# Scores of fourteen attention units on eight 64-row by 32-column tiles instead of two 128-row by 64-column ones

## The chip, the cores and the metric

The kernel runs on one core of one Trainium2 chip. The metric is the time of one execution in microseconds (us), as the median of several runs. One other execution of the same program was profiled; all rows shown here come from it.

## The reference

Four inputs of 576 tokens, eight heads of 64, go through windowed attention and then through two feed-forward layers (512 to 2048 to 512) on the 2304 tokens. Heads 0 to 3 look at the last 32 tokens, heads 4 to 7 at every fourth of the last 128.

```python
rel = pos[:, None] - pos[None, :]
mask_plain = (rel >= 0) & (rel < window)                                   # window 32
mask_dil = (rel >= 0) & (rel < window * dilation) & (rel % dilation == 0)  # dilation 4
scores = np.where(masks, q @ k.T / sqrt(D), -1e9)
attn = exp(scores - max) / (sum + 1e-9);  y = attn @ v      # y: 2304 x 512
h = y @ w_in;   g = where(h > 0, h, exp(min(h, 0)) - 1);   y = g @ w_out
h = y @ w2_in;  g = h * clip(h + 3, 0, 6) / 6;             out = g @ w2_out
```

## The kernel before, in words

**Units.** The attention is cut into 18 units of 128 tokens, all eight heads (`unit`, line 520). A unit has eight blocks `n`: four of the dilated heads (one for each residue), four of the plain heads, each with 32 queries of four heads against a window of 64 keys. A unit is a chain: loads of q, k, v; scores on TensorE into PSUM tile `ps` (`scores`); for units 4 to 17 VectorE adds the mask while it copies to SBUF (`low`), takes the row minimum (`top`), ScalarE exponentiates with the row sums (`expos`), VectorE scales; TensorE turns the result (`turn`, into `pp`); two copies bring it to `pt`; TensorE multiplies with v (`pv`, into `po`); and a copy and a subtraction bring it to `xh`, `xl`, the two halves that the first layer reads (the last six units: one copy to `xw` and a store).

**Zero padding in q.** Heads lie in pairs, a pair's two times 64 dimensions on the 128 partitions. Line 579 issues one matmul for each block and pair `c`: 128 rows, 64 stationary columns (32 queries of the one head with zeros in the other head's rows, then the reverse), 64 moving columns of keys. That is 16 fp32 matmuls in a unit, `c` = 0 on the left half of the array and `c` = 1 on the right half.

**Order of the work.** The kernel is one program written out job by job. `Plan.run` places the jobs: it walks forward in an estimated time, takes for each engine the job that can start first, ties by `key`, and charges each job the cost in its `job(...)` call (scores: 0.071 us x 16 = 1.136). What it decides is fixed in the program: each engine runs its list in order and waits at semaphores. The keys of the first feed-forward layer are spread over three blocks of 512 tokens, whose starts `TB` hold `CFG["AT"]` us for each attention unit (4, 6 and 4 units). The second layer follows with keys counted from `TB[3]`. Units 4 to 7 feed block 1, units 8 to 11 block 2, units 12 to 17 the second layer's first part. All loads and most stores are issued by SyncE's queue.

**PSUM.** Eight banks with names: h0, h1 (the `h` of the first layer), y0 to y3 (its outputs), a0, a1 (attention of units 4 to 17). `ps`, `pp` and `po` of a unit each take one of a0, a1, whichever is free first, and free it when their last reader is done. Each use is a tile of its own in that bank.

**Masks.** GpSimd writes five masks at the start (`make_mask`, `make_masks`). Units whose blocks touch the beginning of an input (4, 5, 9, 13, 14) need more than one and split `low` into runs of blocks with the same mask.

Of the kernel before, what the change touches and what calls it, by code (L numbers as in the profile page):

```python
# [20 lines left out]
P = 128  # L21
# [18 lines left out]
    LAGT=0.23, LAGE=0.07, LAND=1.6,  # L40
    T0=30.0, AT=2.6,
    AHEAD=6,
    LEAD=10.0,
    LAG=12.0,
# [154 lines left out]
def tile_window_attention_two_mlps(  # L199
    ctx: ExitStack,  # L200
    tc: tile.TileContext,
    q_in: bass.AP,
    k_in: bass.AP,
# [40 lines left out]
    minus = at.tile([P, P], BF16, name="minus")  # L244
    mask = at.tile([P, 5, KW], BF16, name="mask")
    NL = 2 * N1
# [273 lines left out]
    def unit(u, key, step):  # L520
# [3 lines left out]
        for n, src, shape, us, dk in (  # L524
            ("q", q_in, [P, 2, NB, KW], 1.3, 0), ("k", k_in, [P, k_in.shape[2]], 1.1, 0),
            ("v", v_in, [P, NB // 2, HH, D], 1.3, CFG["VL"]),
        ):

            pool, ring = (at, n) if not 0 < u < U1 else {
                "q1": (None, "raw"), "q2": (None, "raw"), "k1": (None, "raw")  # L530
            }.get(f"{n}{u}", (w1p, "w1"))

            def load(e, n=n, src=src, shape=shape, pool=pool, ring=ring):
                t[n] = grab(lu[n], shape, F32, f"{n}{u}") if lu[n].tag else take(pool, ring, shape, F32, f"{n}{u}")
                nc.sync.dma_start(out=t[n], in_=src[u])

            ld[n] = job(key - CFG["LEAD"] + dk, load, {"S": 0.42}, (), us, [(RINGS[ring], lu[n])])

        masks = [first_seen(u * QB, S // DIL)] * DIL + [first_seen(u * UN + n * QB, S) for n in range(UN // QB)]
        tags = []  # L540
        for _ in range(3):
            tags.append(bank_tags[0] if u < U1 else "a")
            bank_tags.rotate(-1)
        r = {}

        def bank(k, shape, nm):
            r[nm] = ps.tile(shape, F32, tag=bu[k].tag, name=f"{nm}{u}")
            return r[nm]
# [13 lines left out]
        pe_masks = u < CFG["MPE"]  # L562

        def masked(e):
            pe = bank(0, [P, NB, KW], "ps")
            for n, w, z in runs:
                nc.tensor.matmul(
                    pe[:, n:n + w, :], minus, mask[:, z:z + 1, :].to_broadcast([P, w, KW]), start=(n == 0), stop=False
                )

        def scores(e):
            pe = r["ps"] if pe_masks else bank(0, [P, NB, KW], "ps")
# [69 lines left out]
        def pv(e):  # L642

            po = bank(2, [P, KD, UN], "po")
# [22 lines left out]
        if pe_masks:  # L667
            j0 = job(key - CFG["KM"], masked, {"T": 0.25}, [setup if full else setups], 0, take1)
            bu[0].append(j0)
        j1 = job(  # L670
            key, scores, {"T": 0.071 * 2 * NB},
            [ld["q"], ld["k"], j0 if pe_masks else setups, (LAST["pv"], -9.0) if u == U1 else None],
# [37 lines left out]
        bu[1] += j7  # L710
        j8 = job(key + 0.7, pv, {"T": 0.066 * 2 * NB}, [*j7, ld["v"]], 0, [(RINGS[tags[2]], bu[2])])
        lu["v"].append(j8)
# [51 lines left out]
    def tile1(b, i):  # L764
# [5 lines left out]
        def g1(e):  # L770
            r["h"] = ps.tile([P, T1], F32, tag=hu.tag, name=f"h{b}_{i}")
            gemm1(w_t[0, i, 0], x_t[b], r["h"], i == 0)
# [33 lines left out]
        def g2(e):  # L806
            w, g = w_t[0, i, 1], r["g"]
            for n in range(KD):
                if i == 0:
                    ys[b, n] = ps.tile([P, T1], F32, tag=f"y{n}", name=f"yp{b}_{n}")  # L810
# [279 lines left out]
    def tile_l(t, i):  # L1090
# [13 lines left out]
        def mm(e):  # L1104
            for n in range(KD):
                if i == 0:
                    ys["l", t, n] = ps.tile([P, N1], F32, tag=yu[n].tag, name=f"yl{t}_{n}")
                for s, (a, v) in enumerate(PASSES):
# [30 lines left out]
    def gemm2nd(c, j):  # L1139
# [10 lines left out]
        def mm(k):  # L1150
# [3 lines left out]
            def fn(e):  # L1154
                if b not in r:
                    r[b] = ps.tile([P, N1], F32, tag=bu[b].tag, name=f"c{b}{c}_{j}")
                    if b == "q":
# [119 lines left out]
    def second(c, h, j):  # L1277
# [19 lines left out]
        for n, (k, ka, kb) in enumerate(PASS[h]):  # L1297
# [38 lines left out]
            def mm(e, r=r, k=k, kb=kb, n=n):  # L1336
                if j == 0:
                    for nm in (str(k), HALF[k][0]):
                        if (c, nm) not in half:
                            opened.add((c, nm))  # L1340
                            half[c, nm] = ps.tile([P, 2, EH], F32, tag=mu[nm].tag, name=f"m{c}_{nm}")
                    for i in range(NG):
# [121 lines left out]

    def make_masks(e):
        later(3, QB // 2)

        nc.gpsimd.memset(mask[:, 2], 0.0)
        for h in range(HH):
# [4 lines left out]
            )  # L1474
        nc.gpsimd.memset(mask[:, 4], 1.0)
        nc.gpsimd.affine_select(
            out=mask[:, 4], in_=mask[:, 4], base=WIN + QB // 2 - 1, pattern=[[-1, KW]], channel_multiplier=0, fill=0.0,
            compare_op=ALU.is_ge,
        )
        m = mask[:, 2]  # L1480
        nc.gpsimd.tensor_tensor(out=m, in0=m, in1=mask[:, 4], op=ALU.mult)
        nc.gpsimd.tensor_tensor(out=m, in0=m, in1=mask[:, 0], op=ALU.add)

    def fill(t0, t1):
# [5 lines left out]
        tag = RINGS["h"].take(())  # L1490
        y = ps.tile([P, P], F32, tag=tag, name=f"fill{next(turns)}")
        for _ in range(n):
# [73 lines left out]
def layout(q, k, v, moe_w_in, moe_w_out, moe2_w_in, moe2_w_out):  # L1566
# [11 lines left out]

    r["q"] = np.zeros((nu, 2, D, 2, NB, 2, QB), q.dtype)
    qd = cut(q).reshape(DIL, 2, 2, nu, QB, D).transpose(3, 2, 5, 1, 0, 4)  # L1580
    qp = flat(q).reshape(2, 2, nu, UN // QB, QB, D).transpose(2, 1, 5, 0, 3, 4)
    for e in range(2):
        r["q"][:, e, :, :, :DIL, e] = qd[:, e]
        r["q"][:, e, :, :, DIL:, e] = qp[:, e]
    r["q"] = r["q"].reshape(nu, P, 2, NB, KW)
    kp, kd, vp, vd = before(flat(k)), before(cut(k)), before(flat(v)), before(cut(v))
    r["k"] = np.zeros((nu, P, 2 * (UN + WIN) + 2 * DIL * KW), k.dtype)
    r["v"] = np.zeros((nu, 2, KW, NB // 2, hh, D), v.dtype)
    for u in range(nu):
# [42 lines left out]
```

## Time and profile before

| | |
|---|---|
| median of 3 runs | 829.96 us (829.28 to 830.64) |
| the profiled execution | 829.3 us, of it span of instructions 827.6 us |
| TensorE busy (PE) | 811.6 us, 98% |
| VectorE (DVE) / ScalarE (ACT) / GpSimd (POOL) busy | 636.3 (77%) / 505.5 (61%) / 47.6 us (6%) |
| granted TensorE clock | 1.00 in every stretch asked for |
| DMA | 230.49 MB, 279 GB/s over the span |

PE are matmuls, PEld the loads of their stationary operand, which run beside them. An fp32 matmul leaves two records of each kind. The units lie between 5 and 281 us, the first layer between 29 and 341 us, the second from 330 us on.

### The profile page before, as it was taken

How to read it: one execution, taken by the hardware profiler on the slowest of the kernel's cores; microseconds unless marked ns; L12 is line 12 of the kernel's file. 1: busy time of each engine (PE TensorE's matmuls, PEld its weight loads, DVE VectorE, ACT ScalarE, POOL GpSimd, SP SyncE). 2: the span in 40 equal slices, each digit the busy share in tenths (PEclk: the TensorE clock that was granted, in tenths of full speed). 3: DMA queues.
4: the chain of work that ended last, by engine and by line, in shares of the span. 5: the costliest groups of instructions: out<-in, count | busy, mean ns of one | idle time of the engine just before them, and what ended most of it. 6: DMA issues, size and time to landing. Idle time of an engine off the chain costs nothing.

```text
span 827.6 us, 15806 instructions
## 1 busy us (share of the span) xinstructions
PE 811.6 (98%) x5691; PEld 750.5 (91%) x5691; DVE 636.3 (77%) x1310; ACT 505.5 (61%) x1179; POOL 47.6 (6%) x71
## 2 busy tenths in 40 slices
PE   8899999999999999999999999999999999999998
PEld 7788888888877887999999999999999999999998
DVE  5999898877778787677998675797677896555985
ACT  2999975766676655677786554444555445444452
POOL 2000010001001000100000000100001100002001
PEclk9999999999999999999999999999999999999999
DMA  9999557866888736999779998986999915778323
GB/s 355 408 408 367 195 180 246 271 213 228 261 287 294 243 125 216 397 414 401 266 256 339 392 373 312 400 339 179 343 379 355 389 59 171 255 256 291 96 59 121
DMA packets 89550, 230.49 MB, mean 279 GB/s; under 512 B 9344, under 2 KB 24192, under 8 KB 89472
## 3 DMA queue, kind: packets, MB, share of 16 engines
q1 hardware_dynamic: 89328, 229.35, 77.8%
q8 instruction: 45, 0.74, 0.4%
q14 instruction: 33, 0.27, 0.1%
q10 hardware_dynamic: 144, 0.13, 0.0%
HBM read 163.38 MB, written 66.06 MB: 277 GB/s over the span
## 4 chain that ended last, share of the span: by engine, by line
PE 78%; DMA 10%; DVE 4%; ACT 4%; issue 1%; SPq 1%; DVEq 0%; ACTq 0%
PE m L1353 20%; PE cq L1163 15%; PE h L757 11%; PE yp L812 9%; PE yl L1109 8%; PE cr L1163 7%; PE cp L1163 4%; DMA raw<-in_w_in_dram 3%; DMA w2do<-store__95 2%; ACT s L614 1%; DMA w2do<-stg 1%; PE po L653 1%; PE m_1x L1353 1%; DMA w2di<-store__95 1%; DMA ws_e<-w2de 1%
## 5 line engine op out<-in xcount | busy, mean ns | idle before, releaser
L812 PE MATMUL yp<-ghl,w 128*128 128x512 f32 x576 | 141.0, 393 | 0.0
L812 PEld LDWEIGHTS yp<-ghl,w 128*128 128x128 f32 x576 | 106.6, 188 | 22.6
L757 PE MATMUL h<-xh,w 128*128 128x512 f32 x384 | 125.6, 394 | 0.1
L1163 PE MATMUL cq<-x,ws_i 128*128 128x384 f32 x576 | 113.3, 339 | 0.7 <-ACT t L276 0.6
L1163 PEld LDWEIGHTS cq<-x,ws_i 128*128 128x128 f32 x576 | 100.9, 188 | 1.4 <-ACT t L276 1.1
L1353 PE MATMUL m<-w,gc 128*128 128x256 f32 x792 | 100.2, 281 | 0.0
L1353 PEld LDWEIGHTS m<-w,gc 128*128 128x128 f32 x792 | 97.2, 190 | 0.0
L757 PEld LDWEIGHTS h<-xh,w 128*128 128x128 f32 x384 | 72.0, 188 | 15.5 <-DVE e L790 0.3
L276 ACT CAST gc<-g 128x384 fp32r<-128x384 f32 x96 | 49.2, 514 | 41.8 <-PE m L1353 22.1
L757 PE MATMUL h<-xl,w 128*128 128x512 f32 x192 | 73.3, 389 | 0.0
L276 ACT COPY t<-cq 128x384 f32<-128x384 f32 x96 | 45.7, 476 | 38.9 <-PE cq L1163 38.0
L1209 ACT ACTIVATE g<-t 128x384 f32<-128x384 f32 x72 | 37.8, 525 | 49.0 <-DVE t L1199 49.0
L1109 PE MATMUL yl<-gl,w 128*128 128x384 f32 x384 | 67.4, 334 | 0.0
L1109 PEld LDWEIGHTS yl<-gl,w 128*128 128x128 f32 x384 | 66.7, 188 | 0.0
L279 DVE TENSOR_TENSOR gc<-g,gc 128x384 fp32r<-128x384 f32 x85 | 48.2, 569 | 17.8 <-ACT gc L276 16.6
L276 ACT CAST gc<-gf 128x384 fp32r<-128x384 f32 x72 | 37.0, 514 | 39.7 <-PE m L1353 35.9
L1215 DVE SCALAR_TENSOR_TENSOR g<-g,t 128x384 f32<-128x384 f32 x72 | 40.2, 559 | 26.6 <-ACT g L1209 26.1
L1163 PE MATMUL cr<-x,ws_i 128*128 128x384 f32 x288 | 55.7, 339 | 0.0
L1353 PE MATMUL m<-ws_e,gc 128*128 128x256 f32 x384 | 52.3, 282 | 0.8 <-DMA ws_e<-w2de 0.8
L335 ACT ACTIVATE raw<-raw 128x512 f32<-128x512 f32 x64 | 42.5, 683 | 17.1 <-DMA raw<-in_w_out_dram 11.6
L1199 DVE TENSOR_TENSOR t<-cr,t 128x384 f32<-128x384 f32 x64 | 35.6, 556 | 20.1 <-ACT t L276 17.9
L1163 PEld LDWEIGHTS cr<-x,ws_i 128*128 128x128 f32 x288 | 50.9, 188 | 0.0
(139 smaller groups left out, 1450.6 us busy)
## 6 DMA issues: line engine op xcount, KB each, us to landing
ws_i<-w2di SPq DMA_DIRECT2D x84, 512.0 KB, 5.5
raw<-in_w_in_dram SPq DMA_DIRECT2D x32, 512.0 KB, 8.0
raw<-in_w_out_dram SPq DMA_DIRECT2D x32, 512.0 KB, 6.5
ws_l<-w2dl SPq DMA_DIRECT2D x28, 512.0 KB, 7.3
ws_e<-w2de SPq DMA_DIRECT2D x24, 512.0 KB, 4.3
w2di<-store__95 SPq DMA_DIRECT2D x44, 256.0 KB, 4.8
rhs<-stg SPq DMA_DIRECT2D x28, 384.0 KB, 6.0
x<-rhs SPq DMA_DIRECT2D x28, 384.0 KB, 8.4
```

Of the source, the lines that this page charges most:

```text
L276: (nc.scalar.copy if e == "A" else nc.vector.tensor_copy)(out=out, in_=in_)
L279: ENG[e].tensor_tensor(out=out, in0=in0, in1=in1, op=ALU.subtract)
L335: nc.scalar.activation(out=x, in_=x, func=AF.Prelu, scale=2.0 ** -112, alpha=-2.0 ** 32)
L614: nc.scalar.activation(out=r["s"][:, n, :], in_=x[:, n, :], func=AF.Exp, scale=z, bias=r["mx"][:, n], accum_out=r["sm"][:, n],)
L757: nc.tensor.matmul(h, w[:, a, c * P:(c + 1) * P], x[b][:, c, :], start=n == 0, stop=n == len(steps) - 1,)
L812: nc.tensor.matmul(ys[b, n], w[:, a, n * P:(n + 1) * P], g[:, c, :], start=(i == 0 and s == 0), stop=(i == KF - 1 and s == 2),)
L1109: nc.tensor.matmul(ys["l", t, n], w_t[0, i, 1][:, a, n * P:(n + 1) * P], r["g"][:, v], start=i == 0 and s == 0, stop=i == KF - 1 and s == 2,)
L1163: nc.tensor.matmul(r[b], w[:, a, p * P:(p + 1) * P], x2[c, k, p][:, z, :], start=start and p == 0 and n == 0, stop=p == 1 and n == 2, skip ...
L1199: nc.vector.tensor_tensor(out=r[n], in0=r[b], in1=r[n], op=ALU.add)
L1209: nc.scalar.activation(out=g_t[c, j][:, k, t].rearrange("q i n -> q (i n)"), in_=r[src], func=AF.Relu, bias=3.0)
L1215: nc.vector.scalar_tensor_tensor(out=z, in0=z, scalar=6.0, in1=r[src], op0=ALU.min, op1=ALU.mult)
L1353: nc.tensor.matmul(ms[c, k, i], r["z"][:, a, i * P:(i + 1) * P], w[:, v, :], start=(c, nm) in opened, stop=end and s == 2,)
```

## The change

For units 4 to 17 `scores2`, `low2` and `pv2` take the place of `scores`, `low` and `pv`. Each head's scores are a matmul of its own: 64 rows (that head's dimensions), 32 stationary columns (its 32 queries, no zeros), 64 moving columns, 32 matmuls in a unit. Row half `z` goes with the head of the pair, column quarter `g` with the pair and the block's parity; consecutive matmuls go to the eight tiles (z, g) in turn. The results of the two row halves go to the two banks a0 and a1 at the same partitions, so a unit's scores take both banks at once (a new ring "pair"), half of each. `low2` reads both with one instruction of 512 elements, or, in the five masked units, with four of 128. q of these units has no zeros and is half as large (256 KB in place of 512). Blocks come in another order, so v is laid out in another order and `pv2` writes its 16 matmuls through other strides. GpSimd makes three copies of the first mask and one mixed mask more. All PSUM tiles become areas of one tile `psum_`. The plan is told 0.8 us for the scores (`TS`), 0.45 us more for a masked `low2`, 3.2 us for `make_masks` in place of 2.0, and 2.3 us in place of 2.6 for `AT`.

```diff
-    T0=30.0, AT=2.6,
+    T0=30.0, AT=2.3,
...
-    LEAD=10.0,
+    LEAD=10.0, TS=0.8,
...
+    RINGS["pair"] = Ring([Pair("a0", BANKS["a0"], BANKS["a1"])])
+    psum_ = ps.tile([P, len(BANKS), DM], F32, name="psum_")
...
-            ("q", q_in, [P, 2, NB, KW], 1.3, 0), ...
+            ("q", q0_in, [P, 2, NB, KW], 1.3, 0) if u < U1 else ("q", q_in, [P, 2, NB, QB], 0.65, 0), ...
...
-            tags.append(bank_tags[0] if u < U1 else "a")
+            tags.append(bank_tags[0] if u < U1 else "a" if tags else "pair")
...
+        def scores2(e):
+            pe = r["ps"] = psum_[:, AREA["a0"]:AREA["a0"] + 2, :DM // 2].rearrange("p z (a b) -> p z a b", b=KW)
...
+            for kind in range(2):
+                for m in range(2):
+                    for g in range(2 * 2):
+                        c, n = g // 2, 2 * m + g % 2
+                        w = window(n if kind else DIL + n)
+                        for z in range(2):
+                            rows = slice(z * D, (z + 1) * D)
+                            nc.tensor.matmul(
+                                pe[g * QB:(g + 1) * QB, z, 2 * kind + m, :], t["q"][rows, c, kind * DIL + n, :], w[rows, c],
+                                start=True, stop=True, tile_position=(z * D, g * QB),
+                            )
...
+        def low2(e):
...
+            while n < NB // 2:
+                w = NB // 2 if not any(kinds) else 1
+                m = mask_[:, :w] if w > 1 else mask[:, kinds[n]:kinds[n] + 1]
+                nc.vector.scalar_tensor_tensor(
+                    out=flat(s[:, :, n:n + w]), in0=flat(r["ps"][:, :, n:n + w]), scalar=-SCALE,
+                    in1=m.rearrange("p (a n) k -> p a (n k)", a=1).to_broadcast([P, 2, w * KW]),
+                    op0=ALU.mult, op1=ALU.add,
+                )
+                n += w
...
-            key, scores, {"T": 0.071 * 2 * NB},
+            key, *((scores, {"T": 0.071 * 2 * NB}) if u < U1 else (scores2, {"T": CFG["TS"]})),
...
-            j2 = job(key + 0.1, low, {"D": C["D"](n)}, [j1])
+            j2 = job(key + 0.1, low2 if u >= U1 else low, {"D": C["D"](n) + 0.45 * any(kinds)}, [j1])
...
     def make_masks(e):
+        for n in range(3):
+            nc.gpsimd.tensor_copy(out=mask_[:, n], in_=mask[:, 0])
+        for h in range(HH):
+            rows = slice(h * QB, (h + 1) * QB)
+            nc.gpsimd.tensor_copy(out=mask[rows, 4], in_=mask[rows, 1 - h % 2])
...
-        setups = job(0.0, make_masks, {"P": 2.0})
+        setups = job(0.0, make_masks, {"P": 3.2})
```

## Rows read from the trace of the kernel before

**Rows 1.** The page's first part: busy us (share), instructions, of each engine.
```profile
PE 811.6 (98%) x5691; PEld 750.5 (91%) x5691; DVE 636.3 (77%) x1310; ACT 505.5 (61%) x1179; POOL 47.6 (6%) x71
```
**Rows 2.** Busy time by stretch: length; engines; granted clock; DMA share; GB/s.
```profile
26.00:60.00 34.00, 33.34 (x285) 27.10 (x284) 32.67 (x66) 33.14 (x83) 0.00 (x0) 1.00 1.04 408
60.00:100.00 40.00, 40.00 (x285) 32.55 (x284) 35.70 (x67) 37.72 (x90) 0.00 (x0) 1.00 0.81 290
220.00:285.00 65.00, 62.40 (x469) 50.44 (x468) 48.05 (x106) 44.69 (x132) 5.55 (x7) 1.00 0.83 275
285.00:828.00 543.00, 534.64 (x3458) 523.36 (x3456) 404.52 (x829) 299.14 (x639) 29.41 (x29) 1.00 0.77 277
```
**Rows 3.** PE's waits from 26 to 290 us: total us, times, longest.
```profile
PE po L653 <- DVE pt L276: 1.7, 1, 1.7
PE po L653 <- ACT pt L276: 0.8, 2, 0.4
PE pp L629 <- DVE s L624: 0.5, 2, 0.4
```
**Rows 4.** Line 579 from 28 to 267 us: count; shortest, median, longest ns.
```profile
L579 PE MATMUL ps<-k,q x448: 222/222/270, 28.2 to 266.6; 128*64 128x64 f32 x150
```
**Rows 5.** Timeline around one unit's scores: start us, length us, engine, line.
```profile
74.17 1.01 PEld L579 LDWEIGHTS ps<-k,q 128*64 128x64 f32 x32 [0.35 <-issue]
74.17 1.15 PE L579 MATMUL ps<-k,q 128*64 128x64 f32 x32
...
75.25 0.53 PEld L812 LDWEIGHTS yp<-ghl,w 128*128 128x128 f32 x3
```
**Rows 6.** Timeline of PE, cut at 74.20 us: the burst's first records.
```profile
74.17 0.28 PE L579 MATMUL ps<-k,q 128*64 128x64 f32 x2
```
**Rows 7.** Line 579 in short stretches: PE records in flight (x), then PEld's.
```profile
74.16:74.20 0.04, 0.03 (x2) 0.03 (x2) 1.00 1.25 486
74.20:74.27 0.07, 0.07 (x2) 0.07 (x4) 1.00 1.00 380
74.27:74.30 0.03, 0.03 (x4) 0.03 (x6) 1.00 1.40 546
74.30:74.33 0.03, 0.03 (x4) 0.03 (x6) 1.00 0.85 341
74.33:74.36 0.03, 0.03 (x6) 0.03 (x6) 1.00 1.24 478
```
**Rows 8.** Timeline from 154.5 to 158 us: a unit's end beside the next one's scores.
```profile
154.84 1.15 PE L653 MATMUL po<-pt,v 128*64 128x64 f32 x32
...
155.82 1.10 PE L579 MATMUL ps<-k,q 128*64 128x64 f32 x32
...
156.84 0.68 DVE L660 TENSOR_TENSOR xl<-po,xh 128x512 fp32r<-128x512 f32 x1
```
**Rows 9.** DVE's line 586 by shape: count, busy us, mean ns, idle before.
```profile
L586 DVE SCALAR_TENSOR_TENSOR s<-ps,mask 128x512 f32<-128x512 f32 x9 | 6.1, 683 | 0.9 <-PE ps L579 0.9
L586 DVE SCALAR_TENSOR_TENSOR s<-ps,mask 128x128 f32<-128x128 f32 x2 | 0.6, 277 | 0.0
```
**Rows 10.** Timeline of POOL, the end of the masks.
```profile
7.25 0.30 POOL L1482 TENSOR_TENSOR mask<-mask 128x64 bf16<-128x64 bf16 x1
```
**Rows 11.** DMA issues by line: count, KB each, median us to landing.
```profile
q<-in_q_dram SPq DMA_DIRECT2D x18, 512.0 KB, 6.4
```
**Rows 12.** Timeline: SP's last unit store; the second layer's first matmul.
```profile
280.36 0.53 SPq L302 DMA_DIRECT2D x1d<-xw  x1
...
329.98 1.29 PE L1163 MATMUL cq<-x,ws_l 128*128 128x384 f32 x6 [1.15 <-POOL raw L425]
```
**Rows 13.** PE's longest waits from 324 to 400 us, then from 400 on.
```profile
PE cq L1163 <- POOL raw L425: 1.2, 1, 1.2
...
PE cp L1163 <- DMA ws_i<-w2di: 0.8, 1, 0.8
PE m L1353 <- DMA ws_e<-w2de: 0.8, 1, 0.8
```

More of the change, by code (lines that the diff above doesn't have):

```diff
@@ L70, in __init__, with users @@
         self.tag, self.users = tag, ()
+class Pair:
+    def __init__(self, tag, *slots):
+        self.tag, self.slots = tag, slots
+    @property
+    def users(self):
+        return [u for s in self.slots for u in s.users]
+    @users.setter
+    def users(self, users):
+        for s in self.slots:
+            s.users = users
 class Users(list):
@@ L201, in tile_window_attention_two_mlps @@
     tc: tile.TileContext,
+    q0_in: bass.AP,
     q_in: bass.AP,
@@ L244, in tile_window_attention_two_mlps @@
     minus = at.tile([P, P], BF16, name="minus")
-    mask = at.tile([P, 5, KW], BF16, name="mask")
+    mask_ = at.tile([P, 9, KW], BF16, name="mask")
+    mask = mask_[:, 3:]
     NL = 2 * N1
@@ L268, in tile_window_attention_two_mlps, with area @@
     RINGS["all"] = Ring(list(BANKS.values()))
+    RINGS["pair"] = Ring([Pair("a0", BANKS["a0"], BANKS["a1"])])
+    psum_ = ps.tile([P, len(BANKS), DM], F32, name="psum_")
+    AREA = {n: z for z, n in enumerate(("a0", "a1", "y0", "y1", "y2", "y3", "h0", "h1"))}
+    def area(tag, *shape):
+        x, n = psum_[:, AREA[tag]], 1
+        for z in shape:
+            n *= z
+        if len(shape) == 1:
+            return x[:, :n]
+        return x[:, :n].rearrange("p (a b) -> p a b", b=shape[-1])
     RINGS["ghl"] = Ring([Slot(f"ghl{n}") for n in range(SIZES["ghl"])])
@@ L524, in unit @@
         for n, src, shape, us, dk in (
-            ("q", q_in, [P, 2, NB, KW], 1.3, 0), ("k", k_in, [P, k_in.shape[2]], 1.1, 0),
+            ("q", q0_in, [P, 2, NB, KW], 1.3, 0) if u < U1 else ("q", q_in, [P, 2, NB, QB], 0.65, 0), ("k", k_in, [P, k_in.shape[2]], 1.1, 0),
             ("v", v_in, [P, NB // 2, HH, D], 1.3, CFG["VL"]),
@@ L534, in load @@
                 t[n] = grab(lu[n], shape, F32, f"{n}{u}") if lu[n].tag else take(pool, ring, shape, F32, f"{n}{u}")
-                nc.sync.dma_start(out=t[n], in_=src[u])
+                nc.sync.dma_start(out=t[n], in_=src[u - U1 if src is q_in else u])
             ld[n] = job(key - CFG["LEAD"] + dk, load, {"S": 0.42}, (), us, [(RINGS[ring], lu[n])])
@@ L546, in bank @@
         def bank(k, shape, nm):
-            r[nm] = ps.tile(shape, F32, tag=bu[k].tag, name=f"{nm}{u}")
+            r[nm] = area(bu[k].tag, *shape)
             return r[nm]
@@ L562, in unit @@
         pe_masks = u < CFG["MPE"]
+        plain = [first_seen(u * UN + n * QB, S) for n in range(UN // QB)]
+        kinds = [{(0, 0): 0, (1, 0): 4}[tuple(plain[2 * m:2 * m + 2])] for m in range(2)] + [first_seen(u * QB, S // DIL)] * 2
+        def scores2(e):
+            pe = r["ps"] = psum_[:, AREA["a0"]:AREA["a0"] + 2, :DM // 2].rearrange("p z (a b) -> p z a b", b=KW)
+            r["s"] = take(at, "s", [P, NB, KW], F32, f"s{u}")
+            st = take(at, "st", [P, 2, NB, 1], F32, f"st{u}")
+            r["mx"], r["sm"] = st[:, 0], st[:, 1]
+            for kind in range(2):
[9 more added lines that the diff above has]
+                            )
@@ new lines, in low2 @@
+        def low2(e):
+            flat = lambda x: x.rearrange("p z m k -> p z (m k)")
+            s = r["s"].rearrange("p (z m) k -> p z m k", z=2)
+            n = 0
+            while n < NB // 2:
[7 more added lines that the diff above has]
+                n += w
@@ new lines, in pv2 @@
+        def pv2(e):
+            po = bank(2, [KD, UN], "po")
+            for x in range(NB // 2):
+                z, kind = x // 2, x % 2
+                for g in range(2 * 2):
+                    c, par = g // 2, g % 2
+                    o = po[z * D:(z + 1) * D, 2 * kind + c]
+                    o = o.rearrange("p (i m q) -> p q m i", m=2, q=2) if kind else o.rearrange("p (m q i) -> p q m i", m=2, q=2)
+                    nc.tensor.matmul(
+                        o[:, par], t["v"][:, 2 * kind + par, 2 * c + z, :], pt[:, x, g, :], start=True, stop=True
+                    )
@@ L564, in masked @@
         def masked(e):
-            pe = bank(0, [P, NB, KW], "ps")
+            pe = bank(0, [NB, KW], "ps")
             for n, w, z in runs:
@@ L571, in scores @@
         def scores(e):
-            pe = r["ps"] if pe_masks else bank(0, [P, NB, KW], "ps")
+            pe = r["ps"] if pe_masks else bank(0, [NB, KW], "ps")
             r["s"] = take(at, "s", [P, NB, KW], F32, f"s{u}")
@@ L626, in turn @@
         def turn(e):
-            pp = bank(1, [P, NB // 2, P], "pp")
+            pp = bank(1, [NB // 2, P], "pp")
             for m in range(0, NB, 2):
@@ L642, in pv @@
         def pv(e):
-            po = bank(2, [P, KD, UN], "po")
+            po = bank(2, [KD, UN], "po")
             for m in range(NB // 2):
@@ L710, in unit @@
         bu[1] += j7
-        j8 = job(key + 0.7, pv, {"T": 0.066 * 2 * NB}, [*j7, ld["v"]], 0, [(RINGS[tags[2]], bu[2])])
+        j8 = job(key + 0.7, pv if u < U1 else pv2, {"T": 0.066 * 2 * NB}, [*j7, ld["v"]], 0, [(RINGS[tags[2]], bu[2])])
         lu["v"].append(j8)
@@ L770, in g1 @@
         def g1(e):
-            r["h"] = ps.tile([P, T1], F32, tag=hu.tag, name=f"h{b}_{i}")
+            r["h"] = area(hu.tag, T1)
             gemm1(w_t[0, i, 0], x_t[b], r["h"], i == 0)
@@ L809, in g2 @@
                 if i == 0:
-                    ys[b, n] = ps.tile([P, T1], F32, tag=f"y{n}", name=f"yp{b}_{n}")
+                    ys[b, n] = area(f"y{n}", T1)
                 for s, (a, c) in enumerate(PASSES):
@@ L1106, in mm @@
                 if i == 0:
-                    ys["l", t, n] = ps.tile([P, N1], F32, tag=yu[n].tag, name=f"yl{t}_{n}")
+                    ys["l", t, n] = area(yu[n].tag, N1)
                 for s, (a, v) in enumerate(PASSES):
@@ L1155, in fn @@
                 if b not in r:
-                    r[b] = ps.tile([P, N1], F32, tag=bu[b].tag, name=f"c{b}{c}_{j}")
+                    r[b] = area(bu[b].tag, N1)
                     if b == "q":
@@ L1340, in mm @@
                             opened.add((c, nm))
-                            half[c, nm] = ps.tile([P, 2, EH], F32, tag=mu[nm].tag, name=f"m{c}_{nm}")
+                            half[c, nm] = area(mu[nm].tag, 2, EH)
                     for i in range(NG):
@@ L1474, in make_masks @@
             )
-        nc.gpsimd.memset(mask[:, 4], 1.0)
+        nc.gpsimd.memset(mask[:, 5], 1.0)
         nc.gpsimd.affine_select(
-            out=mask[:, 4], in_=mask[:, 4], base=WIN + QB // 2 - 1, pattern=[[-1, KW]], channel_multiplier=0, fill=0.0,
+            out=mask[:, 5], in_=mask[:, 5], base=WIN + QB // 2 - 1, pattern=[[-1, KW]], channel_multiplier=0, fill=0.0,
             compare_op=ALU.is_ge,
@@ L1480, in make_masks @@
         m = mask[:, 2]
-        nc.gpsimd.tensor_tensor(out=m, in0=m, in1=mask[:, 4], op=ALU.mult)
+        nc.gpsimd.tensor_tensor(out=m, in0=m, in1=mask[:, 5], op=ALU.mult)
         nc.gpsimd.tensor_tensor(out=m, in0=m, in1=mask[:, 0], op=ALU.add)
@@ L1490, in fill @@
         tag = RINGS["h"].take(())
-        y = ps.tile([P, P], F32, tag=tag, name=f"fill{next(turns)}")
+        y = area(tag, P)
         for _ in range(n):
@@ L1577, in layout @@
     before = lambda x: np.concatenate([np.zeros((*x.shape[:-2], WIN, D), x.dtype), x], -2)
-    r["q"] = np.zeros((nu, 2, D, 2, NB, 2, QB), q.dtype)
+    nf = W1[0] // UN
     qd = cut(q).reshape(DIL, 2, 2, nu, QB, D).transpose(3, 2, 5, 1, 0, 4)
     qp = flat(q).reshape(2, 2, nu, UN // QB, QB, D).transpose(2, 1, 5, 0, 3, 4)
+    r["q0"] = np.zeros((nf, 2, D, 2, NB, 2, QB), q.dtype)
     for e in range(2):
-        r["q"][:, e, :, :, :DIL, e] = qd[:, e]
-        r["q"][:, e, :, :, DIL:, e] = qp[:, e]
-    r["q"] = r["q"].reshape(nu, P, 2, NB, KW)
+        r["q0"][:, e, :, :, :DIL, e] = qd[:nf, e]
+        r["q0"][:, e, :, :, DIL:, e] = qp[:nf, e]
+    r["q0"] = r["q0"].reshape(nf, P, 2, NB, KW)
+    r["q"] = np.ascontiguousarray(np.concatenate([qp, qd], -2)[nf:]).reshape(nu - nf, P, 2, NB, QB)
     kp, kd, vp, vd = before(flat(k)), before(cut(k)), before(flat(v)), before(cut(v))
@@ L1593, in layout @@
         r["k"][u] = np.concatenate([z.reshape(P, -1), y.reshape(P, -1)], 1)
-        for n in range(DIL):
-            r["v"][u, n % 2, :, n // 2] = vd[n, :, u * QB:u * QB + KW].transpose(1, 0, 2)
-        for n in range(UN // QB):
+        for n in range(NB // 2):
             z = u * UN + n * QB
-            r["v"][u, n % 2, :, (DIL + n) // 2] = vp[:, z:z + KW].transpose(1, 0, 2)
+            for kind, x in enumerate((vp[:, z:z + KW], vd[n, :, u * QB:u * QB + KW])):
+                if u < nf:
+                    r["v"][u, n % 2, :, (0 if kind else 2) + n // 2] = x.transpose(1, 0, 2)
+                else:
+                    r["v"][u, n // 2, :, 2 * kind + n % 2] = x.transpose(1, 0, 2)
     r["v"] = r["v"].reshape(nu, P, NB // 2, hh, D)
```

## The prediction

> **What bounds the kernel now.** I read the page's busy line first: TensorE's matmuls fill 811.6 of 827.6 us, and no other engine comes near [rows 1]. So the second view is busy time by stretch, for the part where the changed units run. From 60 us on PE is busy through whole stretches; in 26 to 60 us it lacks 0.66 us, in 220 to 285 us 2.6 us, and in the 543 us behind them 8.4 us, at granted clock 1.00 (2.4 GHz) throughout [rows 2]. The reader is to see that the units stand inside an unbroken stream of feed-forward matmuls: what they take from PE, the stream gets later. The third view is PE's waits in that stretch: three lines, all at the turn or at `pv` of a unit, 3.0 us in 5 waits [rows 3]. Scores are not among them. ACT and DVE are close behind early on (37.7 and 35.7 of 40 us from 60 to 100 us), DMA is full from 26 to 60 us [rows 2].
>
> **The scores on PE.** Line 579 leaves 448 records for 14 units [rows 4], 32 in each, two for each of 16 matmuls. One unit's burst begins at 74.17 us and its last record, 0.22 us long [rows 4], ends 1.15 us later, so it starts 0.93 us after the first; the next line's weights are loaded at 75.25 us [rows 5]. The burst occupies PE for 1.08 us, with a tail of 0.15 us behind its last start.
>
> What sets the 0.93 us? Two records are in flight at once: by 74.20 us both have started, together 0.28 us long where one is up to 0.27 [rows 4, 6], so the second starts some 0.01 us after the first. Cut into short stretches, none starts until 74.27, then two, none until 74.33, then two again [rows 7]. The records come in rounds of two, one on each half of the array: the first round lasts about 0.10 us (its weights have to be loaded), the other 14 intervals (0.93 - 0.10) / 14 = 0.059 us each. So a record waits for its own tile; issuing one takes 0.01 us or less.
>
> After the change a unit has 32 matmuls, 64 records, on eight tiles: 8 rounds. A record still streams 64 columns, so I take 0.059 us for a round. Last start: 0.10 + 6 x 0.059 + the lag of the eighth tile behind the first (7 steps of some 0.007 us, estimated from the pair's 0.01) = 0.50 us; with the tail 0.65 us, against 1.08: 0.43 us less. Fourteen units: -6.0 us. These lie on the path that sets the end, since PE is full around them.
>
> The trace holds no 64-row tile, so bounds. If all tiles shared one feed at the present rate, 32 records in 0.93 us or 0.029 each, 64 would take 1.86 us: +0.93 in each unit, +13.0 us. If column quarters ran together but the two row halves did not, or the reverse, there would be 16 rounds again: 0. At best weights of half as many columns also halve the first round: 0.05 x 14 = 0.7 us more, -6.7. I take -6.0, since the two tiles that the trace shows are independent down to 0.01 us.
>
> A rule of the Trainium skill speaks against this (TensorE: Matmul & The Clock Gate, section "Wait — 56ns, not 53.3ns?"): starts of matmuls never come closer than about 25 ns however few columns they have. Here two starts lie within about 10 ns [rows 6], so the trace doesn't agree for records on different tiles. By the rule 64 records would take an estimated 1.6 us and a unit 1.75 us with the tail, +0.67, +9.4 us in all.
>
> **A change of tile shape.** `pv` keeps 128 by 64 tiles. Where scores follow `pv` directly, as at 155.82 us, the earlier burst occupies 155.82 - 154.84 = 0.98 us, not 1.08 [rows 8]: the tail of about 0.1 us is saved because both have one shape. That is so in two of the 14 units. It goes: +0.2 us.
>
> **The pair of banks (a new wait).** Scores now need both a0 and a1, so they stand behind the last reader of `po` of the unit before. In the trace scores of the next unit run at 155.82 us, while the unit before still has `xl` to read from the other bank until 157.52 [rows 8]; after the change they must come at least 1.7 us later. In the plan this is no stall: PE does other work, which stands before the scores in its list. Neither does the later unit miss its use: the last store of a unit is issued at 280.36 us and the second layer starts at 329.98 [rows 12], so 49.6 us lie between them for the preparation of its operands, and delays of a few us fit. What it costs is where the list is wrong: if DVE's `xl` is late, scores wait in PE's queue with all feed-forward matmuls behind them. Turn and `pv` of these units are 28 such places, and cost 3.0 us [rows 3]; 14 more at that rate cost +1.5 us. Bounds: 0, and 14 x 1.7 = 24 us if every one were as bad as the worst.
>
> **Mask and copy on DVE.** Nine units keep one instruction of 512 elements (0.683 us). Five have four of 128 (0.277 each, 1.11 us) in place of two to four of several sizes, which can't take less than one of 512 does: at most 5 x (1.11 - 0.68) = 2.1 us more in all [rows 9]. What hides it is PE's other work, which stands in its list before the unit's turn; if that cover were gone it would cost up to 2.1 us. I take 0. The same answer for the larger `make_masks`: seven small GpSimd instructions of at most 0.3 us behind 7.55 us [rows 10], needed by unit 4's scores at 28.2 us [rows 4]; 0, at most 7 x 0.3 = 2.1.
>
> **q half as large.** 14 x 256 KB less is 3.7 MB of 230.5 [rows 11]; at the 408 GB/s of the full stretch that is 9 us of DMA time. But PE lacks only 0.66 us in that stretch [rows 2], so the gain is between 0 and 0.7 us; I take 0. SyncE issues as many loads as before.
>
> **The plan.** `AT`, `TS` and the 3.2 move keys, up to 14 x 0.3 = 4.2 us by `TB[3]`; the lists of all engines come out anew. No engine's work grows by this, but the waits of PE behind 324 us are set by others: by GpSimd's and DVE's preparation of weights at 328.8 us (1.2 us), by weights landing (0.8 each) [rows 13]. If these don't come earlier with PE, part of the gain is given back there, where DMA is at a share of 0.77 on average [rows 2]. Bounds: 0, and all of the gain. I take +0.5 us, because the loads' keys move with `TB`.
>
> **Sum.** -6.0 + 0.2 + 1.5 + 0.5 = -3.8 us. The profiled execution took 829.3 us, 1.7 of it outside the span: 825.5. The median before is 829.96, 0.66 higher: by that 826.2. I predict 826.0 us.
>
> **Rivals.**
> - *The gain is real but lost behind it* (the burst falls to about 0.65 us, the time stays within 1.7 us). For it: ACT and DVE at 94% and 89% from 60 to 100 us [rows 2], and preparation chains that PE already waits for [rows 13]. Against it: after 285 us PE lacks only 8.4 of 543 us. Time: 829.3 - 6.0 + 5 us of new idle = 828.3, on the median's base 829. Chance 0.16.
> - *Tiles aren't independent*: a common feed of records, bursts of 1.3 to 2.0 us. It decides as soon as a record costs over 0.93 / 64 = 0.0145 us. For it: the trace shows but two tiles, and both in the same rows. Against it: 0.01 us between starts [rows 6]. At the present mean rate +13 us, 843; at half of that excess 836. Chance 0.08; the skill's rule of 25 ns above is of this kind, with its 839.
> - *The pair stalls PE*: the scores are issued too early for `xl`, wait in PE's list, and what ends there is DVE. It passes the gain from 6.0 / 14 = 0.43 us a unit on; the one long wait of now, 1.7 us [rows 3], in every second unit would give +12 - 6 = +6: 835. Against it: the plan knows of the wait, and 23 of the 28 waits of this kind cost nothing. Chance 0.06.
> - *The first layer's order comes out better too*, with fewer waits in 220 to 285 us: up to 3 us more, 822.5. In the forecast's 0.70.
>
> **How the numbers follow.** Forecast 0.70, its own range 822.5 to 828. Faster or slower by over 0.2% (1.7 us, about what a measurement of this kernel can tell from no change): faster 0.70 from the forecast, same 0.16 from the first rival, slower 0.14 from the other two. The range goes from 822 to 832: above it lie the worse halves of the slower cases, some 0.1, below it less.
>
> **What would show it.** Line of `scores2`: 64 records a unit in a burst of about 0.5 us to the last start, 0.65 with the tail; in flight eight at a time; rounds of 0.059 us. Right as to the place if PE's busy time falls by about 6 us and its idle time grows by no more than 2. The pair's cost: waits of PE at the scores' line for DVE `xl` or ACT `xw`, some 1.5 us in all. Wrong if starts come 0.025 us or more apart, if the burst stays at 1.1 us or above, or if PE's idle time after 324 us grows by the gain.

## The result and the profile after

The changed kernel took 839.48 us (median of 6, 836.61 to 840.21) against 830.13 us before (median of 6; the 829.96 above is that of the first three): ratio 1.0108, 95% interval 1.009 to 1.0125. It is 9 us slower; I had forecast 4 us faster. The profiled execution took 839.96 us, its span is 837.9 us.

The page's busy line, which answers to [rows 1]:

```profile
PE 822.5 (98%) x6139; PEld 757.1 (90%) x6139; DVE 637.0 (76%) x1307; ACT 504.0 (60%) x1179; POOL 58.5 (7%) x87
```

PE is busy 10.9 us longer, and its share is unchanged. The lost time is therefore not waiting, it is matmuls. The stretches, as in [rows 2], agree: from 60 to 285 us PE is as full as before or fuller, and from 26 to 60 us it lacks only 0.36 us more.

```profile
26.00:60.00 34.00, 32.98 (x317) 26.75 (x317) 31.92 (x66) 33.30 (x82) 1.32 (x1) 1.00 1.00 369
60.00:100.00 40.00, 40.00 (x348) 32.65 (x346) 34.35 (x62) 36.64 (x79) 1.92 (x2) 1.00 0.76 269
220.00:285.00 65.00, 64.08 (x621) 52.00 (x620) 48.55 (x110) 46.21 (x138) 6.05 (x7) 1.00 0.77 254
285.00:838.00 553.00, 543.16 (x3512) 528.82 (x3510) 407.78 (x832) 296.00 (x636) 31.08 (x31) 1.00 0.76 273
```

So which matmuls? The groups by line answer it. Two lines carry the changed work: 607 (`scores2`) and 636 (`pv2`). First the groups of the changed kernel from 27 to 297 us, then those of the kernel before from 27 to 285 us (columns: count, busy us, mean ns of one, idle before):

```profile
L607 PE MATMUL psum__96<-k,q 64*32 64x64 f32 x896 | 12.0, 224 | 0.9 <-DMA k<-in_k_dram 0.9
L636 PE MATMUL psum__96<-pt,v 128*64 128x64 f32 x448 | 26.6, 225 | 0.0
```
```profile
L579 PE MATMUL ps<-k,q 128*64 128x64 f32 x448 | 15.8, 224 | 0.1
L653 PE MATMUL po<-pt,v 128*64 128x64 f32 x480 | 17.3, 225 | 2.5 <-DVE pt L276 1.7 <-ACT pt L276 0.8
```

The scores fell from 15.8 to 12.0 us with twice the records. But `pv`, with the same 32 records a unit and the same 225 ns each, grew: 26.6 / 14 = 1.90 us a unit against 17.3 / 15 = 1.15 (the 480 are 15 units). That a record's length is unchanged while the group's busy time grows means less overlap. The timeline of a unit's `pv2` and of the matmuls behind it, and the count of its records in flight, in short stretches, show the same:

```profile
193.84 1.90 PE L636 MATMUL psum__96<-pt,v 128*64 128x64 f32 x32
195.67 1.20 PE L888 MATMUL psum__96<-ghl,w 128*128 128x512 f32 x4
```
```profile
193.83:193.93 0.10, 0.09 (x1) 0.09 (x2) 1.00 0.00 0
193.93:193.99 0.06, 0.06 (x2) 0.06 (x3) 1.00 0.00 0
193.99:194.04 0.05, 0.05 (x3) 0.05 (x3) 1.00 0.00 0
```

One record more in each stretch of 0.06 us, where the scores of before put in two [rows 7]. The reader finds the reason in the loops: `pv` ran over heads `h` inside and wrote to half `h % 2`, so neighbours went to different column halves; `pv2` runs over `x` outside with `z = x // 2`, so eight matmuls in a row go to one half, then eight to the other. Each waits for its own tile. The burst occupies PE for 195.67 - 193.84 = 1.83 us, against 1.08 for the scores of before, which have the same 32 records in the same shape [rows 5].

The scores, as in [rows 5] and [rows 7]: the burst, the next line's weights, and records in flight (a record is at least 0.21 us long, so up to the fourth stretch none has ended, and the count is that of all that have started).

```profile
181.44 0.86 PE L607 MATMUL psum__96<-k,q 64*32 64x64 f32 x64
```
```profile
182.23 0.19 PEld L833 LDWEIGHTS psum__96<-xh,w 128*128 128x128 f32 x1
```
```profile
181.43:181.49 0.06, 0.05 (x8) 0.05 (x12) 1.00 0.35 137
181.49:181.55 0.06, 0.06 (x13) 0.06 (x21) 1.00 1.17 341
181.55:181.61 0.06, 0.06 (x21) 0.06 (x27) 1.00 0.40 137
181.61:181.67 0.06, 0.06 (x30) 0.06 (x19) 1.00 0.75 205
181.67:181.73 0.06, 0.06 (x33) 0.06 (x11) 1.00 0.59 205
```

Eight start within 0.05 us, as the eight tiles allow. The burst occupies PE for 182.23 - 181.44 = 0.79 us, not 0.65; before it was 1.08 [rows 5]. That saves 0.29 us a unit, 4.1 us in all.

The waits of PE from 26 to 290 us, as in [rows 3], and the start of the second layer, as in [rows 12]:

```profile
PE psum__96 L607 <- DMA k<-in_k_dram: 0.9, 1, 0.9
PE psum__96 L833 <- ACT xh L304: 0.6, 1, 0.6
PE psum__96 L729 <- ACT pt L304: 0.4, 1, 0.4
```
```profile
336.23 0.94 PE L1239 MATMUL psum__96<-x,ws_l 128*128 128x384 f32 x4 [0.83 <-DMA ws_l<-w2dl]
```

The second layer starts 336.23 - 329.98 = 6.25 us later. The two groups give 14 x (1.90 - 1.15) - 14 x 0.29 = 10.5 - 4.1 = 6.4 us, about as much; the rest of the order is new as well, so the agreement is no proof. Another 4 us of the span (10.3 in all) arise behind that start.

### The profile page after: what moved, and what is told of

Read it like the earlier page. It is cut to its first block, busy times and chain, and to the rows that moved or that the text cites. A ratio compares the mean times of both kernels' runs of the same rounds, so it can differ in the third digit from the quotient of the medians.

```text
span 837.9 us, 16735 instructions
## 1 busy us (share of the span) xinstructions
PE 822.5 (98%) x6139; PEld 757.1 (90%) x6139; DVE 637.0 (76%) x1307; ACT 504.0 (60%) x1179; POOL 58.5 (7%) x87
## 4 chain that ended last, share of the span: by engine, by line
PE 76%; DMA 16%; DVE 3%; ACT 2%; issue 1%; SPq 1%; POOL 0%; DVEq 0%; POOLq 0%; ACTq 0%
PE psum__96 L1239 19%; PE psum__96 L1429 17%; PE psum__96 L833 16%; PE psum__96 L888 15%; PE psum__96 L1185 4%; PE psum__96 L636 3%; DMA ws_i<-w2di 3%; DMA rhs<-stg 2%; DMA ws_e<-w2de 2%; DMA w2di<-store__95 1%; PE psum__96 L607 1%; DMA w2do<-stg 1%; DMA w<-w2do 1%; DMA x<-rhs 1%; PE psum__96 L705 1%
## 5 line engine op out<-in xcount | busy, mean ns | idle before, releaser
L1239 PE MATMUL psum__96<-x,ws_i 128*128 128x384 f32 x1008 | 184.5, 340 | 2.3 <-ACT t L304 1.4
L1239 PEld LDWEIGHTS psum__96<-x,ws_i 128*128 128x128 f32 x1008 | 176.0, 188 | 4.6 <-ACT t L304 2.2
L888 PE MATMUL psum__96<-ghl,w 128*128 128x512 f32 x576 | 141.8, 395 | 0.0
L888 PEld LDWEIGHTS psum__96<-ghl,w 128*128 128x128 f32 x576 | 106.5, 188 | 23.1
L833 PE MATMUL psum__96<-xh,w 128*128 128x512 f32 x384 | 126.4, 396 | 0.6 <-ACT xh L304 0.6
L1429 PE MATMUL psum__96<-w,gc 128*128 128x256 f32 x864 | 108.4, 282 | 0.4 <-DMA w<-w2do 0.4
L1429 PEld LDWEIGHTS psum__96<-w,gc 128*128 128x128 f32 x864 | 105.5, 190 | 0.8 <-issue 0.8
L833 PEld LDWEIGHTS psum__96<-xh,w 128*128 128x128 f32 x384 | 72.0, 188 | 16.3 <-ACT xh L304 0.7
L833 PE MATMUL psum__96<-xl,w 128*128 128x512 f32 x192 | 73.4, 390 | 0.0
L1185 PE MATMUL psum__96<-gl,w 128*128 128x384 f32 x384 | 66.9, 335 | 0.0
```

The lines of the kernel that those rows point to most:

```text
L833: nc.tensor.matmul(h, w[:, a, c * P:(c + 1) * P], x[b][:, c, :], start=n == 0, stop=n == len(steps) - 1,)
L888: nc.tensor.matmul(ys[b, n], w[:, a, n * P:(n + 1) * P], g[:, c, :], start=(i == 0 and s == 0), stop=(i == KF - 1 and s == 2),)
L1185: nc.tensor.matmul(ys["l", t, n], w_t[0, i, 1][:, a, n * P:(n + 1) * P], r["g"][:, v], start=i == 0 and s == 0, stop=i == KF - 1 and s == 2,)
L1239: nc.tensor.matmul(r[b], w[:, a, p * P:(p + 1) * P], x2[c, k, p][:, z, :], start=start and p == 0 and n == 0, stop=p == 1 and n == 2, skip ...
L1429: nc.tensor.matmul(ms[c, k, i], r["z"][:, a, i * P:(i + 1) * P], w[:, v, :], start=(c, nm) in opened, stop=end and s == 2,)
```

## The experiments

Ratios are to the kernel before on the same chip. e1, f3, f4, h2, h3 and h4 do the same work (that of the change with `pv2` alternating) in different orders; e3, f1, f2 and h1 do that of the kernel before. `AT` and `UL` are two numbers of the plan: `AT` is the time that the starts of the first layer's blocks hold for each unit, `UL` the spacing of the keys of units 8 to 17. A smaller key lets a job be placed earlier.

**e1, `pv2` alternating.**

```diff
-            for x in range(NB // 2):
-                z, kind = x // 2, x % 2
-                for g in range(2 * 2):
-                    c, par = g // 2, g % 2
+            for kind in range(2):
+                for gz in range(2 * 2 * 2):
+                    g, z = gz // 2, gz % 2
+                    x, c, par = 2 * z + kind, g // 2, g % 2
```

> The changed kernel with one edit: the loops of pv2 are ordered so that consecutive matmuls alternate between the two column halves, as pv did before; same matmuls, same operands. Theory (the loss is pv2's order: eight matmuls in a row on one column half, so one tile at a time): a unit's 32 records of pv go back from 57 ns each to about 33, 14 x 32 x 0.024 = 10.8 us of PE come back, 839.5 - 10.8 = 828.7 us, and lower if the later phase also gains. Rival (the strided writes of pv2, or the wait for the pair of banks, or the new order of the plan costs the time): 839 us, pv records stay at 57 ns.

828.87 us, 0.9979 (0.9961 to 0.9998). Between it and the changed kernel lie 1.0108 / 0.9979 = 1.29%, 10.7 us; the theory said 10.8. The group of line 636:

```profile
L636 PE MATMUL psum__96<-pt,v 128*64 128x64 f32 x448 | 16.1, 225 | 0.0
```

16.1 / 14 = 1.15 us a unit, as before, with the same strides, banks and plan (the bursts on PE stand in the same order in both traces). The rival falls as an account of these 10.7 us. The start of the second layer:

```profile
324.86 1.30 PE L1239 MATMUL psum__96<-x,ws_l 128*128 128x384 f32 x6 [0.83 <-DMA ws_l<-w2dl]
```

That is 5.1 us earlier than before [rows 12], but the span ends only 0.9 us earlier (826.7 against 827.6). So some 4 us are lost behind this start here too (1.7 of them to a slower clock, see h1), as in the changed kernel: at most a part of its 4 us can come from the order of `pv2`.

**e2, the order alone in the kernel before.**

```diff
-            for m in range(NB // 2):
-                for h in range(HH):
+            order = [(m, h) for m in range(NB // 2) for h in range(HH)]
+            if u >= U1:
+                order.sort(key=lambda x: x[1] % 2)
+            for m, h in order:
```

> The kernel before with one edit: for units 4 to 17 pv issues its eight matmuls of one column half first and then the eight of the other; scores, q, masks, banks and plan are untouched. Theory (order alone costs): pv's records of these units go from 33 to 57 ns, +10.8 us, 830.1 + 10.8 = 840.9 us. Rival (order does not matter, strides or banks do): 830 us.

840.37 us, 1.0121 (1.0095 to 1.0147): +10 us from the order of 16 matmuls alone. The group of `pv`, from 27 to 297 us (15 units, of which 14 are changed), had 17.3 us before:

```profile
L656 PE MATMUL po<-pt,v 128*64 128x64 f32 x480 | 27.7, 225 | 0.6 <-ACT pt L276 0.4 <-DVE pt L276 0.2
```

So the cause of the 10.7 us is shown from both sides.

**e3, the pair of banks in the plan of before.**

```diff
-            tags.append(bank_tags[0] if u < U1 else "a")
+            tags.append(bank_tags[0] if u < U1 else "a" if tags else "pair")
```

> The kernel before with one edit: the plan lets the scores of units 4 to 17 take both banks a0 and a1, so they are placed behind the last reader of the unit before, as in the changed kernel; they still write one bank, and AT and all costs stay. Theory A (the pair only shifts units inside slack): within 1.5 us of 830.1. Theory B (the pair is what delays the second layer, the 4 us that the changed kernel loses behind 336 us): 832 to 835 us.

835.27 us, 1.006 (1.0038 to 1.0081). The size of theory B, at its upper end; but see f1 and f2 for what it means.

**e4, half of the moving columns.**

```diff
-                                pe[g * QB:(g + 1) * QB, z, 2 * kind + m, :], t["q"][rows, c, kind * DIL + n, :], w[rows, c],
+                                pe[g * QB:(g + 1) * QB, z, 2 * kind + m, :QB], t["q"][rows, c, kind * DIL + n, :], w[rows, c, :QB],
```

> The changed kernel with scores2 streaming 32 of the 64 key columns (the other half of the scores is left out). It asks what sets the 0.64 us from first to last start of a burst. If streaming on the tiles does, both halves of the burst shrink by nearly half: about 0.35 us. If the second half of the burst, whose records come 16.7 ns per matmul behind a pause after the 32nd record, is set by how fast instructions reach TensorE, that half stays at 0.28 us with the pause, and only the first half shrinks: about 0.5 us.

One execution, 839.82 us; it can't be told from the changed kernel's 839.48. The burst and the count in flight (a record is 0.19 us long here):

```profile
180.60 0.76 PE L607 MATMUL psum__96<-k,q 64*32 64x32 f32 x64
```
```profile
180.59:180.65 0.06, 0.05 (x7) 0.05 (x11) 1.00 2.06 614
180.65:180.71 0.06, 0.06 (x20) 0.06 (x27) 1.00 1.32 273
180.71:180.77 0.06, 0.06 (x32) 0.06 (x32) 1.00 0.75 273
180.77:180.79 0.02, 0.02 (x32) 0.02 (x18) 1.00 1.99 819
180.79:180.85 0.06, 0.06 (x33) 0.06 (x14) 1.00 0.75 205
```

32 records have started 0.17 us into the burst, where with 64 columns 30 had by 0.23 us; then one more in the next 0.08 us, and the last starts at 0.76 - 0.19 = 0.57 us, against 0.86 - 0.22 = 0.64. With half the streaming the first half shrank by about a third and the rest hardly: 0.32 us for the last 31 records, against 0.35 with 64 columns. So streaming doesn't set the second half. Loading the weights on a tile doesn't either: the first half has the same loads, and its records start twice as fast. Of the causes named, the second theory is left, the pace at which instructions arrive; no run varies that pace, so it is not shown, and the 0.57 us are more than its 0.5.

**f1 and f2, only keys moved in the kernel before** (the first edit is f1, the second f2).

```diff
-    MORE=3, RW=7, RL=0, LL=20.0, PREPL=(60.0, 140.0), UL=14.0, XL=12.0,
+    MORE=3, RW=7, RL=0, LL=20.0, PREPL=(60.0, 140.0), UL=16.7, XL=12.0,
...
-    T0=30.0, AT=2.6,
+    T0=30.0, AT=2.3,
```

> The kernel before with the keys of units 8 to 17 spaced by 16.7 us in place of 14, the pace at which the pair of banks let them go in e3_before_pair (16.68 us), and nothing of the pair. Theory (the pair costs because the last units are done 12 us later, and the preparation of the second layer then collides with its weight loads): like e3, 833 to 836 us. Rival (the cost lies in the pair's order itself, not in the lateness): within 1.5 us of 830.1.

826.75 us, 0.9964 (0.9947 to 0.998): neither the theory's 833 to 836 us nor the rival's 830. The last unit's `pv` begins at 297.6 us, in e3 at 291.3. So units as late as in e3 need not cost anything. But `UL` stands in one more key, that of the first preparation of the second layer's operands (`lds`, line 1520), which f1 moves 10 x 2.7 = 27 us later and e3 left as it was. That this preparation collides with the weight loads in e3 is therefore not refuted.

> The kernel before with AT=2.3 in place of 2.6 and nothing else: only the keys of the plan move, up to 4.2 us, the work is the same. It measures what a new order alone does. My sum put +0.5 us on it: 829 to 831.5. If the order of loads and preparations is what the second layer hangs on, it moves by several us either way.

835.51 us, 1.0072 (1.0046 to 1.0098): not the 829 to 831.5 of my sum, but as much as the pair in e3, and without it. In this profile the second layer loses it. PE's waits from 310 us on (total, times, longest); the first matmuls behind the longest wait; and the stretch from just before them, with the granted clock as the third number from the end:

```profile
PE cq L1163 <- ACT t L276: 7.1, 6, 4.6
PE m L1353 <- DMA ws_e<-w2de: 0.9, 1, 0.9
```
```profile
338.64 2.29 PE L1163 MATMUL cq<-x,ws_l 128*128 128x384 f32 x6 [4.63 <-ACT t L276]
```
```profile
337.20:344.00 6.80, 5.36 (x14) 4.68 (x15) 3.80 (x8) 4.37 (x10) 1.58 (x2) 0.50 1.01 367
```

The wait costs twice. PE stood idle for 4.63 us, and from 337.2 to 344.0 us TensorE was granted a clock of 0.50 (1.2 GHz): six records took 2.29 us there, 1.29 us in the kernel before [rows 12]. By the 5.36 us of busy time at half clock this is an estimated 2.7 us on top of the wait. It is not this profile alone: the mean granted clock of all six executions of f2 lies between 0.995 and 0.998.

So a new order of the same jobs is worth -3 to +6 us, and e3's +5 us can't be put down to the pair as such.

**f3 and f4, e1 with AT=2.6 and AT=2.0.**

> e1_pv_alternate with AT back at 2.6. If the second layer gives back phase one's gain because its keys come earlier than its preparation, later keys keep more of the gain: 825 to 828 us. If the give-back is DMA time that no key moves, 828 to 830.

830.17 us, 1.0014 (0.9992 to 1.0035). Neither expectation's reason holds: later keys kept nothing of the gain.

> e1_pv_alternate with AT=2.0, the other side of f3. Units, preparation and second layer are keyed 4.2 us earlier again. If the keys are already too early, it is slower than e1's 828.9, 830 to 833; if the plan's order is a matter of luck at this size, it lands within 2 us of e1 on either side.

833.94 us, 1.0043 (1.0024 to 1.0062). Both sides of e1's AT are slower, f3 by little; there is no slope.

**h1, the work of before in the plan of the change.** The pair, the keys and all costs of the changed kernel, so that every job has the same engine and place; `scores`, `pv`, q and the tiles of before.

```diff
-    T0=30.0, AT=2.6,
+    T0=30.0, AT=2.3,
-            key, scores, {"T": 0.071 * 2 * NB},
+            key, scores, {"T": 0.071 * 2 * NB if u < U1 else 0.8},
-        setups = job(0.0, make_masks, {"P": 2.0})
+        setups = job(0.0, make_masks, {"P": 3.2})
...
```

> The work of the kernel before in the plan of the changed kernel: the plan is given the pair of banks, AT=2.3, 0.8 us for scores, the higher costs of low and make_masks and the shorter load of q, so that every job stands on the same engine at the same place as in the changed kernel, but scores, pv, q and PSUM tiles are those of before. It takes the plan apart from the work. If the scores' gain (bursts 1.08 to 0.79 us, 14 x 0.29 = 4.1 us) is kept whole, this kernel is 4.1 us slower than e1_pv_alternate's 828.9: 833.0, and the new plan by itself costs 2.9 us. If the gain is lost on the way, it is as fast as e1, 829, and the plan costs nothing. If the new plan is better than the old, it is below 830.

831.9 us, 1.0034 (1.0022 to 1.0047). The plan by itself, the pair included, costs 0.34%, 2.8 us; from here to e1 it is 0.9979 / 1.0034: 0.55%, 4.6 us, by the two intervals some 3 to 6. The bursts stand in the same order on PE in both traces. This step holds the scores' gain and all other new work (q, `low2`, the strides of `pv2`). It agrees with the 4.1 us of the bursts, kept whole within the intervals. The start of the second layer in h1, and a stretch of e1 behind a wait of 2.1 us for `ws_e`:

```profile
330.85 1.30 PE L1180 MATMUL cq<-x,ws_l 128*128 128x384 f32 x6 [1.12 <-DMA ws_l<-w2dl]
```
```profile
595.30:598.70 3.40, 3.40 (x15) 3.40 (x14) 1.90 (x4) 1.40 (x4) 0.00 (x0) 0.50 1.03 398
```

In the profiles e1's second layer starts 6.0 us earlier than h1's (324.86 against 330.85), and 2.4 us of this are lost behind it, an estimated 1.7 of them to 3.4 us at half clock.

**h2, h3, h4: e1 under other keys.** AT=2.6 with UL=16.7; AT=2.3 with UL=16.7; AT=2.6 with UL=15.4. As in f1, `UL` moves the key of `lds` too.

> The changed kernel with pv2 alternating, AT=2.6 and the units' keys spaced by 16.7 us as in f1, which was 3 us faster than the kernel before. If f1's order and the scores' gain add up: 826.8 - 4 = 823. If an order's gain doesn't carry over to another list of jobs: anywhere from 826 to 833, as f2 and f4 moved.

823.92 us, 0.9935 (0.9917 to 0.9954): faster than the kernel before, and than f1 by 0.9935 / 0.9964, 0.29% or 2.4 us. Its page and its PE waits from 310 us on:

```profile
PE 810.6 (99%) x6139; PEld 746.4 (91%) x6139; DVE 633.4 (77%) x1295; ACT 509.7 (62%) x1191; POOL 58.2 (7%) x87
```
```profile
PE psum__96 L1239 <- DMA ws_l<-w2dl: 1.7, 2, 1.3
PE psum__96 L1239 <- ACT t L304: 1.1, 3, 0.6
PE psum__96 L1429 <- DMA ws_e<-w2de: 0.6, 1, 0.6
PE psum__96 L1239 <- DMA ws_i<-w2di: 0.3, 1, 0.3
```

3.7 us of waits, spread over seven places. If f1's gain and the scores' 4.1 to 4.6 us added up, h2 would be that much faster than f1; it is 2.4 us, within the intervals. The two also differ in the order of their jobs, so this is no proof that the gains add; that the time came near the expected 823 is in part the other chip (829.12 us for the kernel before, 829.89 on f1's).

> As h2 with AT=2.3: e1_pv_alternate with the units' keys spaced by 16.7 us. The units go at 16.4 us already, held by the pair of banks, so if only the order of the units counts: within 1.5 us of e1's 828.9. If an order's luck decides: 825 to 834.

830.73 us, 1.0027 (1.001 to 1.0045): over 1.5 us above e1, so the order of the units alone doesn't decide. Its longest wait, and the stretch behind it:

```profile
PE psum__96 L1239 <- DVE x L304: 5.0, 1, 5.0
```
```profile
334.80:341.60 6.80, 6.46 (x19) 6.16 (x20) 5.99 (x14) 3.60 (x8) 0.00 (x0) 0.50 0.31 115
```

As in f2, a long wait at the start of the second layer is followed by 6.8 us at half clock, an estimated 3.2 us; the mean clock of all 12 executions is 0.994 to 0.996, where that of h2's six is 0.999 or 1.000.

> As h2 with keys spaced by 15.4 us. It shows how far the time moves from one order to the next with the same work and nearly the same keys: if smoothly, between f3 (14 us, 830.2) and h2 (16.7 us); if not, the order of loads behind 330 us is what moves it.

829.27 us, 0.9998 (0.9982 to 1.0014). It lies between f3 and h2, as a smooth course would have it, though it can't be told from f3, while h3 (same UL as h2, other AT) is slower than e1: moving both keys isn't smooth. Six orders of the same work lie between 0.9935 and 1.0043.

## Why the prediction was wrong, point by point

- **The step that failed** is the one on the tile shape: "`pv` keeps 128 by 64 tiles", with +0.2 us for it. It priced the shape and put the order of `pv2`'s matmuls at nothing. I had just found that a record waits for its own tile [rows 7] and did not carry this to the other rewritten loop: 16 records on one half and then 16 on the other, each 0.059 us behind the last, are by my own number about 32 x 0.059 = 1.9 us; 1.83 us of PE were measured, in place of 1.08. e1 takes the cost away, e2 makes it alone: 10.7 and 10 us.
- **The +0.2 us itself** rests on a miscount. Scores follow `pv` directly in six of the 14 units of before (155.82, 188.81, 202.40, 215.98, 231.67 and 265.68 us), not in two, and in none of the changed kernel: by the same 0.1 us each it is +0.6.
- **The scores**: right in mechanism, -6.0 us taken, -4.1 us measured in the bursts and -4.6 us in time (h1 to e1). The lag of the eighth tile, 0.05 us, was right (eight starts in 0.05 us). Mis-sized was the time of the later rounds: I let rounds of 0.059 us go on to the end, but that pace holds for the first half of a burst only, and the second half takes 0.4 us in place of 0.24 (e4 says what does not set it). The mean is 0.64 / 63 = 0.010 us a record, under the 0.0145 from which the rival of the common feed would have decided.
- **The rule of 25 ns** between starts, of the Trainium skill (TensorE: Matmul & The Clock Gate, "Wait — 56ns, not 53.3ns?"), would have given an estimated 1.75 us a unit; 0.79 was measured, so the traces don't agree with it for matmuls on different tiles. That its 839 us are close to the measured 839.48 is a coincidence.
- **The pair of banks**: the waits behind `xl` that I priced at +1.5 us are absent; PE's waits before 290 us fell from 3.0 to 1.9 us. The units are delayed by more than "a few us", though: the last store of a unit is issued at 295.01 us, 14.7 us later than before [rows 12].

```profile
295.01 0.53 SPq L330 DMA_DIRECT2D x1d<-xw  x1
```

- **Masks, q and `make_masks`** at 0 show no sign against it: q's 14 loads are 256 KB, and DMA's share in the first stretch fell from 1.04 to 1.00 without gain for PE.
- **The plan**: h1 takes plan, pair and shape together. I had +0.5, +1.5 and +0.2, in all +2.2 us; +2.8 was measured. That the sizes are close is luck, since the waits that I priced are absent, and keys alone moved the time by -3 and +6 us (f1, f2).
- **The first rival**, a gain that is real but lost behind it, had 828.3 to 829 us. With `pv2` alternating its time would have come true: e1 took 828.87, and its gain of 5.1 us at the second layer's start shrank to 0.9 at the end. So without the step that failed the forecast of 826.0 would still have been 2.9 us off.
- **The steps as measured**: +2.8 (plan, before to h1), -4.6 (new work, h1 to e1), +10.7 (`pv2`, e1 to the changed kernel). They add up to the ratio of 1.0108 by construction. Independent of them are the bursts: -4.1 for the scores and +10.5 us for `pv2`.
- **Open**: which link of the order decides. Part of it the profiles show: in f2 and h3 one wait of 4.6 and 5.0 us is followed by 6.8 us at half clock, in h4 and e1 waits of 3.5 and 2.1 us by 3.4 us. f4 and e3 are slow at a granted clock of 1.00, so that is not all, and no run isolates which job comes too late.

## What to carry to other kernels

Small matmuls on tiles are priced by how long each tile is busy, not by their count: list the tile of every matmul in program order, and check every loop that the diff reorders, also those whose instructions stay the same. Where a planner orders the work, compare two versions at the same order too (the old work in the new plan, as h1), since the order alone may be worth more than the change. And look at the granted clock behind each long wait of TensorE: the wait may be only part of its price.

## What the runs showed of the hardware

- In a burst of 64 records on eight tiles the first half starts within some 0.24 us with 64 columns (30 records by 0.23) and 0.17 with 32; the others come at 0.010 to 0.012 us each with either. The Trainium skill gives TensorE a queue of 64 entries (TensorE: Matmul & The Clock Gate, "Architectural detail: the array is 16× 32×32, not 1× 128×128"); 32 loads of weights and 32 matmuls are 64 records, which fits the place of the break if each takes one entry, though no run here changed it.
- 64-row by 32-column tiles ran beside each other in fp32, with the row halves writing two banks: up to eight starts within 0.05 us.
- fp32 records of 64 columns on one and the same 128 by 64 tile start some 0.06 us apart, while two tiles in turn take two in that time: eight matmuls in a row on each half cost 1.83 us in place of 1.08.
- After single waits of TensorE of 2.1 to 5.0 us (e1, h4, f2, h3) the granted clock stood at 0.50 for 3.4 to 6.8 us; six records of 384 columns took 2.29 us then (f2), 1.29 at full clock.
